# Routed attention with a gated FFN on one core: the first batch done in whole pairs, its FFN moved into the second batch, the last weights loaded from step 70

## The chip, the cores and the metric

The kernel runs on one core of a Trainium2 chip. The metric is the device time of one call in microseconds (us), as the median of several executions. A profiled execution gives a span from the first to the last instruction; a timed run of the same execution lies about 1.8 us above it. Ratios between kernels are computed as the mean time of one kernel's fast runs over that of the other's fast runs of the same rounds, so they are not quite the ratio of the medians quoted.

The engines are called by what the profile prints: PE is TensorE (PEld its weight loads), DVE VectorE, ACT ScalarE, POOL GpSimd, and SP the engine that here only issues DMAs. SPq, ACTq and so on are the engines' own sequencers.

## The reference

Four batches of eight heads, 768 tokens, head size 64. Queries and keys are each assigned to the nearest of 16 centroids, and a query attends only to keys of its own cluster. The heads are laid side by side and go through a gated FFN.

```python
q_assign = argmax(q_n @ c_n.T); k_assign = argmax(k_n @ c_n.T)      # 16 clusters a head
mask = q_assign[..., :, None] == k_assign[..., None, :]
attn = softmax(where(mask, q @ k.T / 8, -1e9))
x = (attn @ v).transpose(0, 2, 1, 3).reshape(3072, 512)
out = (sigmoid(x @ w_gate) * (x @ w_val)) @ w_out                   # 512 -> 1536 -> 512
```

## The kernel before

The mask is part of the score matmul: 16 additional rows of the transposed key and query hold the one-hot cluster (key) and a large negative number wherever the cluster differs (query), so the exponential of a masked score is zero. Before a head can be scored, its keys and queries are split into a high and a low half-precision part (tile `hl`), transposed (tile `T`, or `TA` and `TB` in batch 0), multiplied with the centroids (logits `lg`), compared with their maximum (`oh`), and the one-hot rows are transposed and copied into rows 64 to 79 of `T`.

The program is one list of *steps*: one score matmul, one exponential, three value matmuls two steps later. FFN matmuls are pushed in between, and preparation hangs on step numbers.

```python
def run_steps(heads, xT, reserve, xt_ready, lag=8):
    ...
            do_scores(s); pend.append(s)
            if xt_ready and done == lag:
                xt_ready()                        # puts the FFN of the last x into the queue
            if xt_ready and done < lag:
                ffn_run(backlog() / (lag - done + 1))
            else:
                ffn_run(max(0.0, backlog() - reserve) / (total - done))
            if len(pend) > LA:                    # LA = 2
                do_av(pend.pop(0), xT)
            run_bg(step_no[0])                    # what at(step, f) has put here
            step_no[0] += 1
```

Batch 0 is done in halves of its queries: 48 steps with the first three of six query chunks of all heads (`A`), then 48 with the others (`B`). So the FFN of the first 384 tokens can start at step 60.

```python
A_SPLIT, A_TURN, A_LG, A_PICK, A_PLACE, A_V, A_VS = -25, -18, -14, -13, -11, -7, -3
for p in range(1, NP):
    U = 12 * p                                    # first step that uses pair p
    ...  at(U + A_TURN, ...); at(U + A_LG, ...); at(U + A_PLACE, lambda p=p: a_place(p))
at(6, lambda: load_w(1)); at(14, lambda: load_wo(0)); at(20, lambda: load_wo(1))
...
run_steps(heads(0, "A", 6), xA, 0, None)
run_steps(heads(0, "B", 6), xB, 6000, lambda: ffn_block(xA, 0, 384, 0, [0, 1, 2]), lag=12)
prev = lambda: ffn_block(xB, 0, 384, 0, [3, 4, 5])
for b in range(1, B):
    run_steps(heads(b, "all", 12), xT, 7000, prev)        # 96 steps a batch
    prev = lambda xT=xT, b=b: ffn_two(...)                # the FFN of this batch, in the next
```

From batch 1 on, the transposes of `hl` are DMA transposes on SP's queue, behind the loads of later q, k and v:

```python
def pair_prep(b, p, use):                         # use = first step of this pair
    s0 = max(use - 58, 58)
    gap = 10 if s0 == use - 58 else 4
    for e in range(2):
        s = s0 + gap * e
        at(s + gap - 1, lambda e=e: turn((b, 2 * p + e), st["hl", e], tp))     # DMA transpose
        at(s + gap + 9, lambda e=e: lgt(e))                                    # logits on TensorE
```

The softmax here doesn't subtract the row's maximum and nothing guards it: scores larger than these inputs give would overflow.

## Time and profile before

| | before |
|---|---|
| median of 2 runs | 354.27 us (353.21 to 355.34) |
| profiled span | 351.4 us |
| TensorE, ScalarE, VectorE, GpSimd busy | 93, 66, 51, 28% |
| starts of scores 49, 97, 193, 289, and the last | 46.9, 84.5, 143.4, 220.9, 292.2 us |

The starts come from counting score matmuls in ever narrower windows (to 0.4 us). They are the backbone of what follows, because each marks the end of a half or of a batch. (The prediction read them by a coarser search, up to 2 us too early.)

The page of the kernel before cuts the span into 40 slices; each digit is a busy share in tenths, and PEclk the clock granted to TensorE:

```profile
PE   7778889999988899999999989999999999999995
...
PEclk9998999999999999999999999999999999999999
DMA  7999565956796576838556495663312011200102
```

TensorE is nearly full from the fifteenth slice on. The DMA engines are full in the first 35 us and half full up to some 235 us. From the view of the tile `hl`, here are the times from the issue of a DMA transpose to its landing between 40 and 120 us:

```profile
DMA to landing us min/median/max: 3.2/3.5/7.7
```

Keep the 7.7 in mind: it is the worst case of the kernel before.

### The profile page before, as it was taken

The numbers are of one execution on the slowest core, as the hardware profiler recorded it, in microseconds if no ns is written. First come the engines' busy times: TensorE is split into PE (matmuls) and PEld (weight loads), VectorE is DVE, ScalarE is ACT, GpSimd is POOL, SyncE is SP. The second block draws the span as 40 slices with busy tenths as digits, with TensorE's granted clock in tenths as the row PEclk, the third lists the DMA queues.
The fourth block names the chain that finished last, engine by engine and source line by source line (L and its number), as shares of the span: only waits on it lengthen the run. The fifth ranks groups of instructions, "written<-read, shape, count | busy, mean of one in ns | idle before, by whom it ended". The sixth has DMA issues, their size and how long they took to land.

```text
span 351.4 us, 8653 instructions
## 1 busy us (share of the span) xinstructions
PE 326.8 (93%) x3274; PEld 202.2 (58%) x3274; DVE 181.0 (51%) x449; ACT 231.3 (66%) x532; POOL 97.8 (28%) x149
## 2 busy tenths in 40 slices
PE   7778889999988899999999989999999999999995
PEld 2556565665555556566666656566665665565552
DVE  6776456774557576446563647265634232342330
ACT  5466786685887789678867777488776883332330
POOL 4952225213263444503332423324110000000000
PEclk9998999999999999999999999999999999999999
DMA  7999565956796576838556495663312011200102
GB/s 257 338 212 209 89 184 150 196 124 169 196 228 185 112 207 149 230 103 216 103 156 140 147 176 154 153 85 81 67 34 85 32 22 32 83 0 33 60 0 90
DMA packets 82026, 46.46 MB, mean 132 GB/s; under 512 B 60992, under 2 KB 78912, under 8 KB 81984
## 3 DMA queue, kind: packets, MB, share of 16 engines
q1 hardware_dynamic: 77888, 40.96, 45.7%
q0 software_dynamic: 3680, 4.72, 7.7%
q8 instruction: 25, 0.41, 0.5%
q10 hardware_dynamic: 416, 0.23, 0.2%
q14 instruction: 17, 0.14, 0.1%
HBM read 28.34 MB, written 6.29 MB: 99 GB/s over the span
## 4 chain that ended last, share of the span: by engine, by line
PE 72%; DMA 5%; DVE 3%; ACT 3%; issue 2%; POOL 1%; SPq 0%; ACTq 0%; DVEq 0%
PE o L377 18%; PE v L360 16%; PE g L345 15%; PE sc L470 12%; PE av L487 7%; DMA T<-hl 5%; ACT es L475 3%; PE lg L277 2%; DVE hT L365 1%; DVE vs L198 1%; DVE hl L744 1%; DVE t L239 0%; POOL hl L745 0%; PE vs_ps L204 0%; DVE oh L295 0%
## 5 line engine op out<-in xcount | busy, mean ns | idle before, releaser
L475 ACT ACTIVATE es<-sc 128x384 f16<-128x384 f32 x384 | 172.4, 492 | 50.7 <-PE sc L470 31.3
L487 PEld LDWEIGHTS <-es 128*128 128x128 f16 x1152 | 80.2, 98 | 48.9 <-ACT es L475 8.3
L487 PE MATMUL av<-va,es 128*128 128x65 f16 x1152 | 97.9, 194 | 2.7 <-ACT es L475 1.1
L365 DVE SCALAR_TENSOR_TENSOR hT<-th,v 128x384 f16<-128x384 f32 x96 | 52.9, 552 | 74.5 <-PE av L487 45.8
L470 PE MATMUL sc<-T 80*128 80x384 f16 x288 | 86.7, 327 | 0.3 <-DVE hT L365 0.2
L377 PE MATMUL o<-wo,hT 128*128 128x512 f16 x288 | 70.3, 378 | 0.0
L351 ACT ACTIVATE th<-g 128x384 f32<-128x384 f32 x96 | 47.2, 491 | 28.0 <-DVE hT L365 16.2
L360 PE MATMUL v<-xTb,wv 128*128 128x384 f16 x288 | 58.6, 325 | 0.3 <-DVE hT L365 0.3
L345 PE MATMUL g<-xTb,wg 128*128 128x384 f16 x288 | 58.6, 325 | 0.0
L345 PEld LDWEIGHTS <-wg 128*128 128x128 f16 x384 | 37.3, 97 | 24.7 <-issue 3.9
L241 POOL TENSOR_TENSOR xp<-t,rec 128x384 f16<-128x384 f32 x24 | 20.0, 832 | 110.9 <-issue 64.1
L360 PEld LDWEIGHTS <-wv 128*128 128x128 f16 x384 | 37.3, 97 | 22.3 <-issue 1.9
L377 PEld LDWEIGHTS <-hT 128*128 128x128 f16 x288 | 27.8, 97 | 26.1
L745 POOL TENSOR_TENSOR hl<-kraw,hl 128x384 f16<-128x384 f32 x24 | 22.1, 919 | 45.2 <-DVE hl L744 35.5
L470 PEld LDWEIGHTS <-T 80*128 80x128 f16 x288 | 27.7, 96 | 0.6
L239 DVE TENSOR_TENSOR t<-av,sv 128x390 f32<-128x390 f32 x32 | 17.9, 561 | 17.3 <-PE av L487 17.1
L745 POOL TENSOR_TENSOR hl<-qraw,hl 128x384 f16<-128x384 f32 x24 | 21.9, 912 | 12.2 <-DVE hl L744 12.2
L386 ACT ACTIVATE ob<-o 128x512 f32<-128x512 f32 x16 | 9.6, 597 | 22.6 <-PE o L377 22.5
L308 DVE TENSOR_TENSOR lgs<-lg,lglo 128x192 f32<-128x192 f32 x24 | 8.5, 355 | 26.2 <-ACT lglo L283 25.9
L470 PE MATMUL sc<-TA 128*128 128x384 f16 x48 | 15.6, 348 | 2.8 <-DMA TA<-ohT 2.8
L198 DVE TENSOR_REDUCE vs<-vraw 128x128 f16<-128x768 f32 x12 | 17.6, 1470 | 0.0
L384 DVE TENSOR_SCALAR ob<-o 128x512 f32<-128x512 f32 x8 | 5.5, 690 | 21.0 <-PE o L377 21.0
(92 smaller groups left out, 275.7 us busy)
## 6 DMA issues: line engine op xcount, KB each, us to landing
vraw<-in_v_dram SPq DMA_DIRECT2D x16, 384.0 KB, 4.8
out_dram<-ob SPq DMA_DIRECT2D x24, 256.0 KB, 2.2
kraw<-in_k_dram SPq DMA_DIRECT2D x15, 384.0 KB, 3.6
qraw<-in_q_dram SPq DMA_DIRECT2D x12, 384.0 KB, 4.2
wg<-in_moe_w_gate_dram POOLq DMA_DIRECT2D x2, 768.0 KB, 10.4
wv<-in_moe_w_val_dram POOLq DMA_DIRECT2D x2, 768.0 KB, 13.3
wo<-in_moe_w_out_dram POOLq DMA_DIRECT2D x2, 768.0 KB, 11.0
qraw<-in_q_dram SPq DMA_DIRECT2D x7, 192.0 KB, 6.2
```

Of the source, the lines that this page charges most:

```text
L198: DVE.tensor_reduce(s[:, :, 0:64], RAW["v", b, p].rearrange("p h c d -> p h d c"), AX.X, ALU.add)
L239: DVE.tensor_tensor(t, av, sv, ALU.add)
L241: eng.tensor_tensor(x, t[..., 0:64], bcast(r, 64), ALU.mult)
L345: PE.matmul(out=g[:, 0:n], lhsT=wg[fc // WQ][:, dc, fc % WQ, :], rhs=xT[:, dc, t0 : t0 + n], start=(dc == 0), stop=(dc == NDC - 1),)
L351: ACT.activation(th[:, 0:n], g[:, 0:n], AF.Tanh, scale=0.5)
L360: PE.matmul(out=w[:, 0:n], lhsT=wv[fc // WQ][:, dc, fc % WQ, :], rhs=xT[:, dc, t0 : t0 + n], start=(dc == 0), stop=(dc == NDC - 1),)
L365: DVE.scalar_tensor_tensor(hT[:, fc, 0:n], st[0][:, 0:n], 1.0, w[:, 0:n], ALU.add, ALU.mult)
L377: PE.matmul(out=o, lhsT=hT[:, fc, bass.ts(t, 128)], rhs=wo[fc // 6][:, fc % 6, :], start=(fc == 0), stop=(fc == NFC - 1),)
L470: PE.matmul(out=sc.rearrange("p (c t) -> p c t", t=128), lhsT=s["k"], rhs=s["q"], start=True, stop=True,)
L475: ACT.activation(es, sc, AF.Exp, scale=SCALE)
L487: PE.matmul(out=av[:, s["c0"] + i, :], lhsT=s["es"][:, bass.ts(i, 128)], rhs=VA[b, p][:, e, s["j"], :], start=(first and i == 0), stop=(la ...
L745: POOL.tensor_tensor(hl[:, :, 64:128], r, hl[:, :, 0:64], ALU.subtract)
```

## The change

The intent: do batch 0 like the other batches, head by head with all 768 queries, so that a pair has 24 steps for the preparation of the next one and not 12. Its FFN has then to wait for batch 1. The output weights, not needed until the middle of batch 1, are loaded late to keep the early transfers short. Cut to its core:

```diff
-    hlp = pool("hl", 3)
-    tp = pool("T", 7)
-    tap = pool("TA", 4)
-    tbp = pool("TB", 4)
+    hlp = pool("hl", 5)
+    tp = pool("T", 9)
 ...
-    for p in range(1, NP):
-        U = 12 * p
+    for p in range(1, NP):
+        U = 24 * p
+        for i in range(4):
+            at(U - 19 + i, lambda x=(2 * p + i % 2, 6 * (i // 2), 6): turn_pe([x], DVE))
+        at(U - 14, lambda p=p: a_logits(p))          # now 48 matmuls in one block
+        at(U - 11, lambda p=p: a_place(p))           # pair 1 too: by DMA copies
-    at(6, lambda: load_w(1))
-    at(14, lambda: load_wo(0))
-    at(20, lambda: load_wo(1))
+    at(4, lambda: load_w(1))
+    for i in range(4):
+        at(70 + 6 * i, lambda i=i: load_wo(i))
 ...
-        s0 = max(use - 58, 58)
-        gap = 10 if s0 == use - 58 else 4
+        s0, gap = max(use - 58, 42), 10
-            at(s + gap + 9, lambda e=e: lgt(e))
+            at(s + gap + 12, lambda e=e: lgt(e))
-                at(max(use - 76, 48 + 4 * p), ...load...)
+                at(max(use - 76, 30), ...load...)
 ...
-    run_steps(heads(0, "A", 6), xA, 0, None)
-    run_steps(heads(0, "B", 6), xB, 6000, lambda: ffn_block(xA, ...), lag=12)
-    prev = lambda: ffn_block(xB, 0, 384, 0, [3, 4, 5])
+    run_steps([(24, first_steps)] + heads(0)[2:], x0, 0, None)
+    prev = lambda: ffn_two((x0, 0, 384, 0, [0, 1, 2]), (x0, 384, 384, 0, [3, 4, 5]))
```

## The prediction

> **What bounds the kernel now.** I count progress in attention steps: a score matmul (128x384), its exponential on ScalarE, three value matmuls. There are 384 of them, 96 a batch. In the windows view of the score line I looked for the times at which the 48th, 96th, 192nd, 288th and last score matmul start (a few records are missing): about 45.5, 82.5, 142, 220 and 292 us. The windows view cut there:
>
> ```profile
> core 0: us, PE busy (x) PEld busy (x) DVE busy (x) ACT busy (x) POOL busy (x), PEclk, DMA share, GB/s
> 0.00:12.60 12.60, 9.19 (x82) 4.46 (x82) 8.10 (x27) 6.05 (x10) 7.18 (x18) 1.00 0.88 296
> 12.60:45.50 32.90, 26.39 (x431) 20.06 (x430) 20.52 (x49) 21.39 (x49) 14.60 (x22) 0.95 0.94 183
> 45.50:82.50 37.00, 34.57 (x403) 22.59 (x400) 25.52 (x70) 27.45 (x66) 12.06 (x15) 1.00 0.65 157
> 82.50:142.00 59.50, 53.75 (x612) 33.87 (x611) 35.78 (x92) 47.92 (x118) 23.80 (x35) 1.00 0.76 191
> 142.00:220.00 78.00, 75.88 (x761) 47.15 (x758) 42.88 (x109) 57.60 (x134) 24.78 (x37) 1.00 0.63 154
> 220.00:292.00 72.00, 71.97 (x692) 44.55 (x691) 31.62 (x74) 54.65 (x126) 14.61 (x23) 1.00 0.31 67
> 292.00:351.40 59.40, 55.06 (x314) 29.56 (x310) 16.55 (x30) 16.21 (x32) 0.82 (x1) 0.99 0.12 44
> ```
>
> The rows: start; first halves of batch 0 (no FFN beside them); second halves (FFN of the first halves); batch 1 (FFN of the second halves only); batches 2 and 3 (a whole FFN each); the last FFN. The last three are TensorE's; the three before them are mixed.
>
> A busy sum overstates a pipelined TensorE, so I take start-to-start times. First the chain of waits, which cuts pieces where the next begins; then the timeline of ScalarE; then that of TensorE:
>
> ```profile
> 53.01 0.16 PE sc L470
> 84.18 0.28 PE av L487 x9
> 294.28 6.04 PE o L377 x28
> ```
>
> ```profile
> 48.95 4.03 ACT L475 ACTIVATE es<-sc 128x384 f16<-128x384 f32 x9 [0.18 <-PE av L487]
> ```
>
> ```profile
> 30.78 0.25 PE L487 MATMUL av<-va,es 128*128 128x65 f16 x3
> 32.52 0.32 PE L470 MATMUL sc<-TA 128*128 128x384 f16 x1 [1.49 <-DMA TA<-ohT]
> ...
> 32.93 0.25 PE L487 MATMUL av<-va,es 128*128 128x65 f16 x3
> 33.02 0.65 PE L327 MATMUL oh_ps<-identh,oh 128*128 128x128 f16 x6
> 33.47 0.52 PE L470 MATMUL sc<-TA 128*128 128x384 f16 x1
> ```
>
> - A step costs TensorE 0.16 + 3 x 0.031 = 0.25 us.
> - An FFN matmul of 512 columns costs 6.04 / 28 = 0.216 us; four gate or value matmuls cost 4 x 0.163 = 0.65 us (the same 0.16 us for 384 columns). An FFN of 384 tokens is 24 x 0.65 + 36 x 0.216 = 23.4 us, of a batch 46.8 us.
> - An exponential is listed at 492 ns, but exponentials overlap: nine in 4.03 us with a last one of 0.49 is (4.03 - 0.49) / 8 = 0.44 us, and the runs of three in 1.25 us elsewhere give (1.25 - 0.49) / 2 = 0.38. I use 0.385 as the floor.
>
> So without FFN work ScalarE sets the floor (0.385 against 0.25), and with a batch of FFN spread over 96 steps TensorE does: 96 x 0.25 + 46.8 = 70.8 us, plus 2.4 us of routing logits. Measured: 72 and 78. The first halves took 32.9 / 48 = 0.69 us a step, far over both floors: preparation for three pairs is packed into the first 24 steps, and twice TensorE waited about 1.4 us for the copy of the one-hot rows (last fence). Score matmuls after that wait took 0.52 instead of 0.33 us for some 3 us.
>
> **What the Trainium skill says.** "TensorE: Matmul & The Clock Gate", Part 1, says that a quiet window drops the array to half clock and sustained work restores it within about 3.4 us. The trace agrees in kind: the granted clock was 0.82 in 30 to 35 us, behind that wait. "DMA: Bandwidth & Descriptors", Issuing engines are not separate DMA queues, says DMAs from any engine share the same 16 engines. The trace agrees: the 24 KB copies to TA took 4.7 us to land while weights were arriving, the same copies to T 1.8 us later. "Perfetto Trace Analysis", Optimization Strategy, advises interleaving regimes bound by different engines. That speaks against the change, which takes FFN work away from ScalarE-bound steps; batch 1 of the kernel before shows room to take it back.
>
> **The change part by part.** Instruction counts come from comparing the two instruction streams.
>
> 1. TensorE work hardly changes: 12 output transposes and 9 one-hot transposes go, 21 x 0.056 = 1.2 us. All scores, logits and key/query transposes stay.
> 2. VectorE loses eight final multiplies of 0.586 us (4.7 us), four output copies of 0.35 and four one-hot copies of 0.35 (2.8 us). The multiplies go to GpSimd at 0.83 us each (6.6 us). The first halves' output transposes go from TensorE to DMA (median 2.8 us to landing, no longer hidden by a lag of 12 steps but of 8).
> 3. Preparation is thinner: each pair now has 24 steps. One pair costs TensorE 24 x 0.25 + 24 transposes x 0.056 + 48 logit matmuls x 0.026 + 0.34 (one-hot turn) + 0.34 (value sums) = 9.3 us, and ScalarE 24 x 0.385 = 9.2 us. Both floors meet, and the work is bursty with only two scores ahead (0.77 us): the 48 logits in one block, 1.2 us, leave ScalarE dry for about 0.6 us, and transposes on four successive steps cost about 0.5 us more. I estimate 10.8 us a pair (0.45 a step), near the 0.41 to 0.49 of the undisturbed stretches before.
> 4. The first pair costs more: weights are still landing from 11 to about 30 us, and the second pair's one-hot copies, asked for at step 13 (about 19 us), need some 4.7 us, against 11 steps = 4.7 us less the turn before them. I allow 1.7 us more for it, then 1.5 us for a spell of half clock. The last pair has no successor in its batch to prepare: 10.3 us. Batch 0: 12.5 + 10.8 + 10.8 + 10.3 + 1.5 = 46 us. The first score starts at about 13 us (0.3 us of additional small VectorE instructions). So step 96 comes at 59 us instead of 82.5.
> 5. Against this, FFN not yet done: the second halves did 23.4 less a reserve of 6, 17.4 us. In batch 1 FFN work rises from 23.4 + 6 - 7 = 22.4 to 46.8 - 7 = 39.8 us.
> 6. Batch 1 before took 59.5 us for 24 + 22.4 + 2.4 = 49 us of TensorE work, because most steps carried no FFN. Now 24 + 39.8 + 2.4 = 66.2 us, plus the loss of batch 2 (78 - 73.2 = 4.8), plus a bubble at its start: the last pair's multiply and transpose take about 0.75 + 0.9 + 0.3 + 3.2 = 5.2 us after step 98, the first gate matmul stands six steps (2.4 us) later and nothing is in the queue to fill: 3 us. Sum 74 us.
> 7. Batches 2 and 3 and the end: unchanged, 78 + 72 + 59.4.
>
> Span: 59 + 74 + 78 + 72 + 59.4 = 342.4 us. A run lies 1.8 us over the profiled span (353.22 against 351.4), the median another 1: about 344.5 us, 2.8% less. Put differently: before, step 192 came at 142 us; now at 133.
>
> Later weights (step 70, some 45 us) cost nothing: the first output matmul comes past the middle of batch 1. They free the early transfers of 3 MB of 9.4, which is part of why I allow only one late copy.
>
> **The rivals.**
> - Batch 0 keeps its pace of 0.69. Then step 96 is at 13 + 66 = 79 us and the span 362: slower by 3%. For it: VectorE and GpSimd are fuller in the second half of batch 0, where I count 20 us of VectorE and 22 us of GpSimd work for batches 0 and 1 in 54 steps (23 us), and their queues are in order. Against: in 40 to 50 us before, the pace was 0.5 with half of that preparation, and the packed first 24 steps are gone. At 0.60 a step the change only breaks even.
> - Batch 0 runs at the floor, 0.40, and batch 1 loses no more than batch 3 did (nothing): step 96 at 52 us, batch 1 at 69, time about 332. Against: TensorE and ScalarE floors coincide, which seldom leaves no bubbles.
> - The gain comes and is eaten: step times in batch 0 are shorter, so leads counted in steps shrink in us. Key/query transposes for batch 1 have 13 steps = 5.9 us against a median of 3.3 us on the transfer plus GpSimd's backlog. If four of these eight waits cost 1.5 us each, the time is about 350: same.
>
> **Range and chances.** The uncertain terms are the pace of batch 0 (0.42 to 0.53 a step, -3 to +8 us) and the loss in batch 1 (-4 to +5 us). Combined: 337 to 354. The 2% line is 347.2 us, 2.7 above my figure, so faster 0.6, same 0.36, slower 0.04.
>
> **What would show it.** Step 96 (the first score on batch 1) at 57 to 62 us; ScalarE busy 75 to 90% from 14 to 59 us, most idle time ended by scores; a TensorE wait on the one-hot copies near step 24 and the clock dipping behind it; a gap of 2 to 4 us in front of the first gate matmul; batch 1 of 71 to 77 us with TensorE busy over 95% of it; rows from batch 2 on as before. The prediction is wrong if step 96 comes after 66 us, or if batch 1 stays over 80 us.

## The result

The changed kernel took 379.33 us (379.03 and 379.63) against 354.27: a ratio of 1.0707 (95% interval 1.0565 to 1.0850). It is slower by 7%, outside the predicted range of 337 to 354, and the side was wrong too.

The windows view of the changed kernel, cut at the same steps (start, batch 0, batches 1, 2, 3, the end; columns as in the prediction):

```profile
0.00:13.50 13.50, 9.58 (x82) 5.03 (x82) 8.38 (x31) 5.95 (x10) 4.97 (x16) 0.87 0.87 300
13.50:83.20 69.70, 47.93 (x716) 33.02 (x714) 36.26 (x84) 42.23 (x101) 36.09 (x49) 0.88 0.87 169
83.20:167.30 84.10, 72.74 (x721) 44.68 (x720) 42.98 (x106) 55.57 (x130) 24.82 (x37) 0.94 0.64 146
167.30:246.10 78.80, 76.43 (x753) 47.15 (x752) 44.03 (x110) 56.75 (x132) 24.75 (x36) 1.00 0.66 147
246.10:318.70 72.60, 71.59 (x684) 44.23 (x681) 32.11 (x74) 54.78 (x127) 14.62 (x23) 1.00 0.27 64
318.70:377.50 58.80, 54.95 (x310) 29.54 (x308) 16.45 (x30) 16.18 (x32) 0.83 (x1) 0.99 0.12 44
```

The last three rows are within 1.3 us of those before (77.5, 71.3 and 59.2 us at the same marks). Nearly all of the loss lies before step 192 (23.9 of 26.1 us of span). Step 96 came at 83.2 us, hardly sooner than the 84.5 before, though batch 0 now carries no FFN at all, and batch 1 took 84.1 us in place of 58.9. In batch 0 no engine was full (TensorE 69%, ScalarE 61%, VectorE 52%, GpSimd 52%): it was bound by waits.

Up to step 72 the changed kernel was even ahead (57.7 against 63.2 us), though with no FFN work done, of which the kernel before had begun its own at step 60. Then this happened. From its timeline, issues on SP's and GpSimd's queues and TensorE's next work (start, length, engine, line, operation):

```profile
57.44 0.80 POOL L146 DMA_DIRECT2D wo<-in_moe_w_out_dram  x1
57.49 0.57 SPq L111 DMA_DIRECT2D kraw<-in_k_dram  x1
...
58.12 0.47 SPq L111 DMA_DIRECT2D qraw<-in_q_dram  x1
...
58.64 0.46 SPq L111 DMA_DIRECT2D vraw<-in_v_dram  x1
...
59.22 5.89 SPq L252 DMA_TRANSPOSE T<-hl  x1
...
60.27 0.80 POOL L146 DMA_DIRECT2D wo<-in_moe_w_out_dram  x1
...
63.57 0.78 POOL L146 DMA_DIRECT2D wo<-in_moe_w_out_dram  x1
65.20 3.06 SPq L489 DMA_TRANSPOSE xTb<-xp  x1
...
75.50 0.50 PE L268 MATMUL lg<-cm,T 128*128 128x32 f16 x12 [11.94 <-DMA T<-hl]
...
75.84 0.48 PE L462 MATMUL sc<-T 128*128 128x384 f16 x1
```

Within 7 us three loads of output weights (384 KB each as landed), a q, k and v load (384 KB each) and a DMA transpose were issued. The logits of step 84 need that transpose, and TensorE stood still in front of them for 11.94 us; the scores behind them, for which the profile lists no wait of their own, started only after them. The issue of that transpose itself held SP's queue for 5.89 us (the median of these issues is 1.42), so the transpose of x behind it was issued late as well. The score behind it ran at 0.48 us, a sign of a lowered clock. The two windows around it, and the landing times of the tile `hl` for 40 to 120 us:

```profile
57.00:63.50 6.50, 5.83 (x71) 2.98 (x71) 3.81 (x9) 6.01 (x18) 5.49 (x8) 1.00 1.02 217
63.50:75.50 12.00, 0.06 (x2) 0.00 (x0) 0.00 (x0) 0.51 (x2) 0.85 (x2) 0.59 1.34 154
```

```profile
DMA to landing us min/median/max: 3.2/3.3/16.2
```

In the second window every engine stood still while the DMA share was the higher of the two (1.34; a share above 1 means that the counted times of packets overlap on an engine) and what was moved the lower (154 GB/s). The median transpose was as before; the worst took 16.2 us in place of 7.7. A second such wait came at the first gate matmul of batch 1, where my prediction had a bubble of 3 us, with the last load of output weights (81.5 us) and another set of q, k and v loads (80.7 to 82.3 us) just ahead of the transpose of x:

```profile
94.78 0.48 PE L336 MATMUL g<-xTb,wg 128*128 128x384 f16 x1 [7.81 <-DMA xTb<-xp]
```

A third, smaller one stood where the prediction had put it, at step 24:

```profile
30.50 0.32 PE L462 MATMUL sc<-T 128*128 128x384 f16 x1 [3.17 <-DMA T<-ohT]
...
31.62 0.51 PE L462 MATMUL sc<-T 128*128 128x384 f16 x1
```

### The profile page after: what moved, and what is told of

It reads as the page before. It is cut to its first block, busy times and chain, and to the rows that moved or that the text cites. A ratio compares the mean times of both kernels' runs of the same rounds, so it can differ in the third digit from the quotient of the medians.

```text
span 377.5 us, 8579 instructions
## 1 busy us (share of the span) xinstructions
PE 333.2 (88%) x3253; PEld 203.6 (54%) x3253; DVE 180.2 (48%) x432; ACT 231.5 (61%) x531; POOL 106.1 (28%) x160
## 4 chain that ended last, share of the span: by engine, by line
PE 65%; DVE 7%; DMA 2%; issue 1%; ACT 1%; POOL 0%; DVEq 0%
PE v L351 16%; PE g L336 16%; PE o L368 16%; PE sc L462 11%; PE av L479 6%; DMA xTb<-xp 2%; DVE hT L356 2%; DVE vs L189 1%; PE lg L268 1%; DVE oh L286 1%; DVE t L230 1%; DVE hl L705 1%; ACT th L342 1%; DVE mx L280 0%; DVE lgs L299 0%
## 5 line engine op out<-in xcount | busy, mean ns | idle before, releaser
L462 PE MATMUL sc<-T 80*128 80x384 f16 (+1 forms) x384 | 119.8, 333 | 4.6 <-DMA T<-ohT 3.2
L479 PEld LDWEIGHTS <-es 128*128 128x128 f16 x1152 | 80.4, 99 | 62.4 <-ACT es L467 13.5
L479 PE MATMUL av<-va,es 128*128 128x65 f16 x1152 | 99.5, 196 | 2.9 <-ACT es L467 1.1
L336 PE MATMUL g<-xTb,wg 128*128 128x384 f16 x384 | 79.0, 327 | 8.4 <-DMA xTb<-xp 7.8
L351 PE MATMUL v<-xTb,wv 128*128 128x384 f16 x384 | 78.9, 327 | 0.5 <-DVE hT L356 0.2
L232 POOL TENSOR_TENSOR xp<-t,rec 128x384 f16<-128x384 f32 x32 | 26.8, 838 | 147.5 <-issue 96.2
L351 PEld LDWEIGHTS <-wv 128*128 128x128 f16 x384 | 37.6, 98 | 23.0 <-issue 2.8
L462 PEld LDWEIGHTS <-T 80*128 80x128 f16 (+1 forms) x384 | 37.5, 98 | 3.8 <-issue 3.3
L268 PE MATMUL lg<-cm,T 128*128 128x32 f16 x288 | 11.0, 177 | 12.7 <-DMA T<-hl 12.7
L274 ACT COPY lglo<-lg 128x192 f32<-128x192 f32 x24 | 7.7, 321 | 17.2 <-PE lg L268 17.2
```

The lines of the kernel that those rows point to most:

```text
L232: eng.tensor_tensor(x, t[..., 0:64], bcast(r, 64), ALU.mult)
L336: PE.matmul(out=g[:, 0:n], lhsT=wg[fc // WQ][:, dc, fc % WQ, :], rhs=xT[:, dc, t0 : t0 + n], start=(dc == 0), stop=(dc == NDC - 1),)
L351: PE.matmul(out=w[:, 0:n], lhsT=wv[fc // WQ][:, dc, fc % WQ, :], rhs=xT[:, dc, t0 : t0 + n], start=(dc == 0), stop=(dc == NDC - 1),)
L462: PE.matmul(out=sc.rearrange("p (c t) -> p c t", t=128), lhsT=s["k"], rhs=s["q"], start=True, stop=True,)
L479: PE.matmul(out=av[:, s["c0"] + i, :], lhsT=s["es"][:, bass.ts(i, 128)], rhs=VA[b, p][:, e, s["j"], :], start=(first and i == 0), stop=(la ...
```

## The experiments

All ran beside the kernel before on the same chip in each set; ratios are to it. The table gives starts of the scores that follow 24, 48, 72, 96, 192 steps, from each run's profile.

| kernel | median us | ratio | 24 | 48 | 72 | 96 | 192 |
|---|---|---|---|---|---|---|---|
| before | 354.27 | 1 | 32.8 | 46.9 | 63.2 | 84.5 | 143.4 |
| changed | 379.33 | 1.0707 | 30.5 | 43.9 | 57.7 | 83.2 | 167.3 |
| wo_mid | 368.26 | 1.0352 | 32.5 | 51.1 | 65.2 | 80.6 | 156.5 |
| wo_memset | 361.03 | 1.0130 | 29.2 | 42.0 | 55.7 | 71.7 | 147.6 |
| loads_early | 372.07 | 1.0432 | 30.8 | 44.9 | 59.3 | 81.9 | 158.1 |
| before_wo_late | 359.40 | 1.0113 | 31.5 | 44.3 | 61.9 | 88.4 | 147.6 |
| wo_post | 360.91 | 1.0215 | 30.5 | 42.9 | 57.0 | 72.7 | 149.3 |
| post_direct | 358.28 | 1.0080 | 26.3 | 39.0 | 51.8 | 68.1 | 147.0 |
| post_spread | 362.69 | 1.0252 | 30.5 | 43.6 | 57.7 | 74.0 | 152.2 |
| before_ffn_moved | 365.64 | 1.0342 | 33.5 | 47.2 | 61.9 | 78.0 | 155.8 |
| post_leads | 354.64 | 1.0006 | 26.9 | 39.7 | 52.8 | 67.8 | 146.3 |
| post_lag14 | 352.77 | 0.9925 | 27.2 | 40.0 | 53.1 | 67.5 | 145.3 |
| post_lag20 | 352.87 | 0.9941 | 26.9 | 39.7 | 52.8 | 67.5 | 147.0 |

(In the kernel before and its variants step 48 ends the first halves. Medians of the kernel before in the later sets were 354.6 to 355.9 us. Each row is one profile, and its first score starts anywhere from 12.2 us, in before_wo_late, to 14.8 us, in wo_mid: a difference of about a microsecond between two rows can come from there.)

### The late weights: wo_mid, wo_memset, loads_early, before_wo_late

Theory 1: the late output weights starve the transposes. Its rivals: the q, k and v loads do (2), or the transposes are too dense by themselves (3).

```diff
-        at(70 + 6 * i, lambda i=i: load_wo(i))
+        at(24 + 2 * i, lambda i=i: load_wo(i))                         # wo_mid
+        at(70 + 6 * i, lambda i=i: POOL.memset(wo[i], 0.0))            # wo_memset: wrong on purpose
-    at(max(use - 76, 30), ...load...)
+    at(max(use - 90, 30), ...load...)                                  # loads_early
-    at(14, lambda: load_wo(0)); at(20, lambda: load_wo(1))
+    at(58, lambda: load_wo(0)); at(64, lambda: load_wo(1))             # before_wo_late, in the kernel before
```

> The changed kernel with the four output-weight loads at steps 24 to 30 in place of 70 to 88, all else the same. Theory 1 (the late weight loads share the DMA engines with the key/query transposes for batch 1 and starve them): the 12 us TensorE wait in front of the logits goes below 3 us, step 96 comes at about 70 instead of 82 us, time 358 to 366 us. Theory 2 (the q/k/v loads of batch 1, issued just ahead of the transposes on the same queue, are what holds them): the wait stays at 8 us or more, time over 372 us. Theory 3 (the transposes are simply too dense at the quicker pace of batch 0): the wait stays as well.

> Wrong result on purpose: the output weights are not loaded but set to zero by GpSimd at the same steps 70 to 88. It takes the transfers away altogether and leaves everything else in place. Theory 1: no wait of over 3 us at the logits, and the wait of the first gate matmul on the transposed x falls from 7.8 us to about 4; time 356 to 364 us, a few us below the kernel with the loads moved. Theories 2 and 3: at least 8 of the 12 us stay, time over 370 us.[...]

> The changed kernel with the q/k/v loads of batches 1 to 3 issued 14 steps earlier (90 instead of 76 steps ahead of use), output weights still from step 70. The load at step 68, directly ahead of the blocked transpose, moves to 54. Theory 1: the logits still wait 6 us or more, time 370 to 379 us. Theory 2: the wait falls below 4 us, time under 368 us.

> The kernel before with its two output-weight loads at steps 58 and 64 in place of 14 and 20, where its own transposes for batch 1 begin. Theory 1: TensorE waits for transposes grow by 4 to 12 us between 55 and 90 us, time 358 to 367 us. If lateness of these loads does no harm by itself (theories 2, 3): within 3 us of 354, or even quicker because the early copies to TA land sooner.

Without the transfers (wo_memset) the waits shrink as theory 1 has it. From the list of waits between 12 and 110 us of wo_memset (idle us in total, times, longest):

```profile
PE lg L268 <- DMA T<-hl: 2.9, 3, 1.9
...
PE g L336 <- DMA xTb<-xp: 0.7, 1, 0.7
```

The 11.94 us became 1.9 at most, the 7.81 became 0.7, and step 96 came at 71.7 in place of 83.2 us. The result was wrong, as intended. So the weights at steps 70 to 88 are a cause. loads_early left them where they were and moved the q, k and v loads away. Its waits in the same window:

```profile
PE lg L268 <- DMA T<-hl: 7.9, 3, 4.7
PE sc L462 <- DMA T<-ohT: 6.0, 4, 3.3
```

The longest logits wait fell to 4.7 us, with another of 3.0 (theory 2 said below 4, theory 1 at least 6), and the time to 372.07 us, a ratio of 1.0432 (theory 1 said 370 to 379). But step 96 came only 1.3 us sooner (81.9): the waits on the one-hot copies grew from 3.2 to 6.0 us. Of the 9.2 us gained at step 192, 7.9 were won in batch 1, where the wait at the first gate matmul was gone. The slowest transpose of `hl` between 40 and 120 us took 16.2 us with both kinds of load, 8.9 with the q, k and v loads earlier, and 6.1 without the weights. So the two kinds together made the long transpose; for the time, taking the weights away helped far more. Whether the same weights, loaded from another queue than GpSimd's, would harm as much was not tested.

The remedy is not simply an earlier place. wo_mid moved the same loads into a quieter stretch (issued at 31 to 38 us); its time was a miss for theory 1 (358 to 366 expected, 368.26 measured), for the logits' waits shrank to 2.1 us in all, but the one-hot copies of the third pair now met the weights and a q, k and v load:

```profile
PE sc L462 <- DMA T<-ohT: 7.6, 2, 4.6
```

The 4.6 us are theirs, at step 48; the other 3.0 are the wait at step 24 that the changed kernel has too. The 24 steps from 24 to 48 took 18.6 us there, against 13.4 in the changed kernel. In the kernel before, late weights did harm too: steps 48 to 96 took 44.1 in place of 37.6 us, with 4.1 us of TensorE waits on key/query transposes in 55 to 90 us, where the kernel before has none (theory 1 said 4 to 12 more). The first halves, now without these loads, took 32.1 in place of 34.3 us from their first score, so that the whole lost only 1.1%.

### A better place for the weights, and what else is lost: wo_post, post_direct, post_spread

```diff
-        at(70 + 6 * i, lambda i=i: load_wo(i))
+        at(106 + 4 * i, lambda i=i: load_wo(i))                        # wo_post and the other post_ kernels
-            at(U - 11, lambda p=p: a_place(p))
+            at(U - 11, lambda p=p: (a_place_direct if p == 1 else a_place)(p))   # post_direct
-        at(U - 14, lambda p=p: a_logits(p))
+        for i in range(4):
+            at(U - 16 + i, lambda p=p, i=i: a_logits_part(p, i))       # post_spread, on wo_post
```

> The changed kernel with its four output-weight loads at steps 106 to 118, behind batch 0, all weights loaded and the result right. Theory (late weights starve the key/query transposes only because they fall into the quick steps of batch 0): as without any load, step 96 at 71 to 73 us, no TensorE wait on a transpose of over 3 us, time 358 to 364 us. Rival (the weights hurt wherever transposes run): the wait of about 10 us moves into batch 1, time 368 to 378 us.

> As the kernel with loads at steps 106 to 118, and the second pair's one-hot rows placed by VectorE in place of the DMA copies that TensorE waits 2.7 to 3.2 us for at step 24. If that wait and the half clock behind it cost their full length: 4 us quicker than its sister, 354 to 360 us. If VectorE's additional four placements (about 2 us) or ScalarE's backlog eat it: within 1.5 us of the sister.

> As the kernel with loads at steps 106 to 118, and the 48 logit matmuls of a pair of batch 0 in four blocks of 12 on four successive steps in place of one block. If bursts on TensorE with only two scores ahead are what keeps batch 0 at 0.53 to 0.57 us a step: ScalarE's 0.84 us gap behind each block vanishes, 3 x 0.8 = 2 to 3 us quicker. If the pace is set by the sum of the work: under 1 us.

wo_post behaves as if there were no weights to load: step 96 at 72.7 us, 360.91 us, result right. Against the changed kernel that is 1.0707 to 1.0215: the place of these loads cost about 4.9 points of the 7.1, some 17 us (the two intervals leave 11 to 23; the profiles differ by 18.0 at step 192). Yet its transposes were still slow where they met the weights:

```profile
DMA to landing us min/median/max: 3.2/4.6/11.3
```

No TensorE wait came of the 11.3 us: its list of batch 1 has no wait on a key/query transpose. What hurt here was a slow transfer with too little time in front of it, not a slow transfer alone.

post_direct removes the one-hot copy at step 24, and steps 1 to 24 end at 26.3 in place of 30.5 us. Of these 4.2 us 0.9 is a first score that started earlier (12.3 against 13.2 us), so wait and slow spell cost about 3.4. 2.3 us were still there at step 192, and the median fell by 2.6 us: between the two expectations, 4 us and under 1.5.

post_spread is a miss for my theory of bursts. The gap behind the block is plain in the changed kernel's timelines of TensorE and of ScalarE:

```profile
36.55 1.35 PE L259 MATMUL lg<-cm,T 128*128 128x16 f16 x48
```

```profile
38.18 1.25 ACT L467 ACTIVATE es<-sc 128x384 f16<-128x384 f32 x3 [0.84 <-PE av L479]
```

Yet spreading the 48 matmuls over four steps made nothing quicker (362.69 against 360.91 us, overlapping intervals), and ScalarE's gap did not vanish: one of 0.93 us stands a little behind the spread blocks. So this gap can't be taken out alone; what sets the pace of these stretches is not shown.

### The FFN taken out of batch 0, alone: before_ffn_moved

```diff
-    run_steps(heads(0, "B", 6), xB, 6000, lambda: ffn_block(xA, 0, 384, 0, [0, 1, 2]), lag=12)
-    prev = lambda: ffn_block(xB, 0, 384, 0, [3, 4, 5])
+    run_steps(heads(0, "B", 6), xB, 0, None)
+    prev = lambda: ffn_two((xA, 0, 384, 0, [0, 1, 2]), (xB, 0, 384, 0, [3, 4, 5]))
```

> The kernel before, halves kept, but the FFN of the first halves is also run in batch 1 (both halves there, one after the other), so the second halves carry none. It does one part of the change alone: taking FFN work from batch 0. If that is neutral, as my prediction had it (step 96 some 13 us earlier, batch 1 some 14 us longer): within 4 us of 354. If work taken from ScalarE-bound steps is simply lost because the weight and load traffic, not the engines, paces batch 0: step 96 less than 6 us earlier, 360 to 368 us.

The halves, the weights and the steps of the preparation are those of the kernel before. (Left out here: the two x tiles become one, and the preparation takes its PSUM buffers from the pool of the FFN's outputs up to step 96 in place of 66, as in the changed kernel.) It cost 3.4%, as the second expectation had it. The windows view of this kernel (first halves, second halves, batch 1):

```profile
12.60:47.20 34.60, 26.85 (x452) 20.20 (x453) 20.88 (x53) 22.66 (x51) 15.02 (x23) 1.00 0.94 189
47.20:78.00 30.80, 23.32 (x291) 14.64 (x290) 20.13 (x57) 21.67 (x52) 12.13 (x15) 0.83 0.68 175
78.00:155.80 77.80, 71.10 (x717) 44.31 (x715) 42.51 (x106) 55.31 (x130) 23.81 (x35) 0.96 0.67 155
```

The second halves without FFN took 30.8 us; with it they had taken 84.5 - 46.9 = 37.6 us. So 17.4 us of FFN work (the prediction's estimate; 96 gate and value and 13 output matmuls, as counted in the trace before, make 18.5 by the same costs) cost only 6.8 us of time there. Three things play into this, and their shares are not separated. The FFN filled waits: without it the second halves ran at 30.8 / 48 = 0.64 us a step, with no engine over 76% busy. The granted clock was 0.83 without and 1.00 with it. And steps without FFN are shorter in time, so leads counted in steps are too: two logits waited 3.0 us for their transposes here, where the kernel before has no such wait. In batch 1 the same work cost 77.8 - 58.9 = 18.9 us, about its full length, but one such wait is in that as well (the longest in batch 1 of the kernel before was 1.4):

```profile
87.97 0.50 PE L277 MATMUL lg<-cm,T 128*128 128x32 f16 x12 [5.31 <-DMA T<-hl]
```

Step 96 came 6.5 us earlier, step 192 12.4 us later.

### Leads in steps: post_leads, after_leads

```diff
-    at(max(use - 76, 30), ...load...)                 s0, gap = max(use - 58, 42), 10
+    at(max(use - 82, 24), ...load...)                 s0, gap = max(use - 64, 36), 10
-            at(s + gap + 12, lambda e=e: lgt(e))      s = s0 + 2 * gap + 14
+            at(s + gap + 18, lambda e=e: lgt(e))      s = s0 + 2 * gap + 20
-        at(use - 10, lambda: st.update(f=v_sum(b, p)))
+        at(use - 14, lambda: st.update(f=v_sum(b, p)))
```

post_leads has this on top of post_direct, after_leads on the changed kernel as it was.

> As the kernel with loads at steps 106 to 118 and the second pair placed by VectorE, and six more steps of lead between the key/query transpose of batches 1 to 3 and its logits, four more for the value sums. If the last 24 steps of batch 0 are at 0.68 us a step because leads counted in steps are too short in time at this pace (waits on the transposes and on the value sums): 3 to 5 us quicker than its sister, 353 to 356 us, the TensorE waits on transposes before step 96 under 1 us in all. If the engines' own queues (GpSimd, VectorE) set that pace: the waits move to other instructions, within 1.5 us.

> The changed kernel with the longer leads alone (six steps more between a key/query transpose of batches 1 to 3 and its logits, loads and transposes starting six steps earlier), output weights still at steps 70 to 88 and the second pair still copied by DMA. If leads in steps were the cause and the weights only made it visible: the 12 us wait shrinks below 4 us, time below 365 us. If the transposes are really starved (16 us from issue to landing): six steps are 2.5 us, the wait only shrinks by 2 to 5 us or moves to the one-hot transposes and copies behind, 370 to 377 us.

post_leads took 354.64 us (1.0006): 1.0080 to 1.0006 against its sister, in the expected size. It was not won where I expected it, though. Step 96 came only 0.3 us sooner (1.2 us counted from the first score, which started later here), and one logits wait of 2.5 us stayed; batch 2 shrank from 79.2 to 75.6 us (steps 192 to 288 in the two profiles). Waits on transposes were not the cause there: the sister's list for 147 to 226 us has none on TensorE. Its largest is three waits for the sums of the values, 1.4 us together, whose lead this kernel lengthens too, and they are gone in post_leads; the rest of the 3.6 us is not explained. And the first gate matmul now waited longer for x:

```profile
PE g L336 <- DMA xTb<-xp: 6.5, 1, 6.5
```

The weights are in this as well. A step is a place in each engine's program, and GpSimd had reached its part of step 106 when TensorE came to the gate matmul of step 104: the first weight load left 0.3 us behind the transpose of x.

```profile
70.91 1.66 SPq L489 DMA_TRANSPOSE xTb<-xp  x1
...
71.17 0.80 POOL L146 DMA_DIRECT2D wo<-in_moe_w_out_dram  x1
```

That transpose took 7.0 us to land. In wo_post, where the load followed 2.6 us behind, it took 4.3.

after_leads took 369.35 us in the median, and 1.0397 in fast runs, just under the 370 to 377 expected of a starved transpose. Its only profile fell into a slow run, so I take from it only a kind and no difference: one wait of 16.2 us on such a transpose was still there. Six more steps of lead, some 2.5 us, did not remove it. Where this kernel gained is not shown.

### The wait at the first gate matmul: post_lag14, post_lag20

```diff
-        run_steps(heads(b), xT, 7000, prev)
+        run_steps(heads(b), xT, 7000, prev, lag=14 if b == 1 else 8)   # or 20; on post_leads
```

> As the kernel with longer leads, and the first FFN work of batch 1 put 14 in place of 8 steps behind its start, so that the score matmuls of six more steps stand in front of the first gate matmul that waited 6.5 us for the last transposed x of batch 0. If that wait is a loss of its full length: 2 to 3 us quicker, 351 to 353 us. If the steps put in front only take ScalarE time that FFN work would have filled: within 1 us of 354.6.

> The same with 20 steps. If the wait of 6.5 us vanishes in full: 4 to 5 us quicker than the kernel with longer leads, 349 to 351 us, and then quicker than both kernels of the case by 1%. If the steps without FFN cost as much as the wait: 354 to 356 us.

With 14 steps the wait fell from 6.5 to 2.7 us:

```profile
PE g L336 <- DMA xTb<-xp: 2.7, 1, 2.7
```

The time fell to 352.77 us over 20 runs, a ratio of 0.9925 (0.9895 to 0.9955). With 20 steps the wait was gone from the list, and the time was the same (0.9941), between the two expectations. That would fit if the steps put in front without FFN work cost what the wait had cost; it is not shown. Both kernels give right results and are quicker than both kernels of the case, by 0.6 to 0.75%. That is clear of noise and small.

### The kernel before, patched: before_direct, before_reserve, before_both

```diff
-            at(U + A_PLACE, lambda p=p: a_place(p))
+            at(U + A_PLACE, lambda p=p: a_place_direct(p))             # before_direct
-        run_steps(heads(b, "all", 12), xT, 7000, prev)
+        run_steps(heads(b, "all", 12), xT, 3500, prev)                 # before_reserve; both in before_both
```

> The kernel before, with the one-hot rows of its third and fourth first halves also placed by VectorE in place of the DMA copies that TensorE waits 1.5 and 1.3 us for. If such a wait costs its length and a spell of half clock, as it did in the changed kernel: 3 to 5 us quicker, 349 to 352 us. If VectorE's extra 1.2 us a pair eats it: within 1 us of 354.

> The kernel before with 3.5 in place of 7 us of FFN kept back at the end of batches 1 to 3. Batch 1, where TensorE has some 10 us to spare, does 3.5 us more of it and the end 3.5 us less. If waits in batch 1 are filled by any FFN work, as the kernel with the FFN moved suggests (17.4 us of FFN beside the second halves cost them only 6.8 us): 2 to 3 us quicker. If the short reserve opens bubbles at the batch starts: same or slower.

> Both edits of the two kernels above. If they are independent: the sum, 5 to 7 us quicker than before, 347 to 350 us, and so quicker than both kernels of the case.

None brought the gain hoped for: 355.65 us (1.0019, 0.9985 to 1.0052), 356.38 us (1.0025, 0.9977 to 1.0072), and 358.93 us (1.0113, 1.0035 to 1.0192, four runs). For the first two the other branch came true; the third is a plain miss. In before_direct the copies' waits were gone, but the first halves ended at 48.5 in place of 46.9 us: ScalarE, which places one of the four, waited 8.8 us for VectorE's placing in 12 to 50 us (4.1 before), and TensorE 4.3 us for exponentials (0.3 before). What was worth 2.6 us with 24 steps a pair is worth nothing with 12. That the two edits together are slower than either alone is not clear of noise.

## Why the prediction was wrong, point by point

The profiled span came out 35.1 us over the predicted 342.4. By the starts of the table, 18.0 are the late weights (step 192 in the changed kernel against wo_post), 13.5 the pace of batch 0 without them, 2.6 batch 1 without them, and the rest small. (A slip besides: 342.4 + 1.8 + 1 is 345.2 us, not 344.5.)

**"Later weights (step 70, some 45 us) cost nothing" failed.** This was the largest error. I asked only when the weights were needed, not what they would meet: the overlap with other transfers was missing. wo_post measures it: 1.0707 to 1.0215, some 17 us of the 25 lost. wo_memset and loads_early show the mechanism: weights and q, k, v loads together delayed one transpose to 16.2 us, TensorE stood behind it for 11.94 us, and then behind x for 7.81 us. The other half of that step held: before_wo_late shows that early transfers without these weights were worth some 2 us in the first halves. The copies that I had seen slowed while weights arrived (4.7 against 1.8 us) were the warning, and I used it for step 24 only.

**Steps 5 and 6, moving FFN work, were not neutral.** Alone, I expected the move to bring step 96 some 13 us sooner and to lengthen batch 1 by some 14. In before_ffn_moved step 96 gained 6.5 us and batch 1 lost 18.9. I had priced steps without FFN from the floors of TensorE and ScalarE; the second halves without FFN were bound by waits, at 0.64 us a step. The cost in batch 1 I had about right (74 us predicted; 77.8 there, 76.6 in wo_post). The sentence of the Trainium skill that I set against the change ("Perfetto Trace Analysis", Optimization Strategy, interleaving regimes) was borne out in direction, and I argued it away with the room in batch 1.

**Steps 3 and 4, the pace of batch 0, were mis-sized.** Predicted 0.45 us a step besides what I allowed for the start and the clock, 46 us in all. In wo_post, without the late weights, batch 0 took 72.7 - 13.2 = 59.5 us, 0.62 a step: 17.3, 12.4, 14.1 and 15.7 for its quarters against 12.5, 10.8, 10.8 and 10.3 (and 1.5 for the clock). The wait at step 24 and the slow spell behind it were foreseen, at 3.2 us together; post_direct shows about 3.4. The excess of the last quarter coincides with batch 1's preparation; longer leads took only some 1.3 us of it (16.3 us in post_direct, 15.0 in post_leads), so what paces it is open. The bursts of logits, to which I gave 0.6 us a pair, were no separable cost.

**The sum.** FFN moved out of batch 0: a loss of 3.4% (before_ffn_moved). From there to wo_post: 1.0342 to 1.0215, a gain of 1.2% (4.5 us between the fast runs of one set, with a 95% interval of 1 to 8). Weights from step 70 in place of 106: 1.0215 to 1.0707, a loss of 4.8%. The middle term is a difference of two kernels and not one edit: whole pairs, but also longer leads and no output weights in the first 30 us, and the last alone was worth some 2 us to the first halves in before_wo_late. So whether the thinner preparation, the idea of the change, won time by itself is not shown; if it did, the two other parts lost several times that.

**What held.** Batches 2, 3 and the end were unchanged within 1.3 us. A wait at step 24 and a gap in front of the first gate matmul were there. The third rival, that leads counted in steps shrink in time, named the right kind of wait, but sized it at 1.5 us each, four of them, and so at 350 us: one alone was 11.94. It also names what before_ffn_moved shows with no weights near, 3.0 and 5.3 us of such waits. The first rival had the length of batch 0 nearly right (step 96 at 79 us). Its reason, full queues of VectorE and GpSimd, is not shown: in wo_post both were 76% busy in 43 to 57.5 us, but 54 and 37% in the slower stretch from 57.5 to 73.

## What to carry to other kernels

When a load is moved, look at what shares the DMA engines at the new place, and at which engine will wait behind the slowest of those transfers, and with how much time in front of it; "needed much later" is not the same as "free now". Before work is taken out of a stretch, find out whether it fills waits there: time it by taking it away, not by its length. Leads that are counted in steps have to be checked again whenever a change alters how long a step lasts.

## What the Trainium skill lacked or had wrong

- "DMA: Bandwidth & Descriptors", Issuing engines are not separate DMA queues, says that DMAs interleave on the same 16 engines. It has no figure for what a transfer suffers that an engine waits for. Here a DMA transpose with a median of 3.3 us took 16.2 us behind q, k, v loads and beside weight loads, and the DMA engines moved less in that window (154 GB/s) than just before it (217 GB/s).
- "TensorE: Matmul & The Clock Gate", Part 1, ties the drop of the clock to an idle window of about 3.4 us; of shorter idling between groups of matmuls it says only that it can make the clock oscillate, without a length. Here waits of 3.17 us, and in the kernel before 1.49 us, were followed within 1.2 us by scores of 0.51 and 0.52 us in place of 0.33. A wait shorter than the window was enough in a stretch where TensorE had other gaps.
- "Perfetto Trace Analysis", Optimization Strategy, advises interleaving regimes without saying how much it can be worth. Here FFN work of an estimated 17.4 us cost 6.8 us in a stretch full of waits, and 18.9 us in batch 1, one wait of 5.3 us included.
